# Transposing the queries by the DMA crossbar instead of TensorE, with tokens reordered and each head's means in its own 32 columns

## The chip, the cores and the metric

The kernel runs on one core of one Trainium2 chip. The metric is the device time of one execution, in microseconds (us). Before the change it is 233.38 us (median of 2 runs, 232.68 to 234.07). A ratio of two kernels is the mean time of one kernel's fast runs over that of the other's fast runs of the same rounds, so it is not quite the ratio of the medians quoted. A run counts as slow when it is over 1.5% above the fastest run of the same kernel.

The engines are called PE (TensorE, matmul), PEld (its weight loads), DVE (VectorE), ACT (ScalarE), POOL (GpSimd) and SP (SyncE; here it only issues DMA transfers).

## The reference, cut to what matters

```python
# q, k, v: (8 batches, 8 heads, 576 tokens, 64); phi: (8, 8, 576, 32)
a   = softmax of phi over the tokens            # 32 memories per head
k_m = einsum('bhsm,bhsd->bhmd', a, k)           # means of k
v_m = einsum('bhsm,bhsd->bhmd', a, v)           # means of v
x   = softmax(scale * q @ k_m^T) @ v_m          # attention over 32 memories
# heads side by side: x is (8, 576, 512); x_prev is x moved on by one token
xk  = mu_k * x + (1 - mu_k) * x_prev
xr  = mu_r * x + (1 - mu_r) * x_prev
out = sigmoid(xr @ w_r) * (relu(xk @ w_k)**2 @ w_v)    # 512 -> 1024 -> 512
```

Two things matter. The scores need q with the 64 features on the partitions, while the load brings it with tokens on the partitions, so q has to be transposed. And x_prev needs the previous token, so the order in which tokens lie in the columns decides which pieces are subtracted.

## The kernel before

Order is fixed by hand. The channel mix works through 9 chunks of 512 tokens, each of 16 groups of matmuls (8 groups of keys, called pk in the program; 4 of gates, pr; 4 of values, pv). The steps of the attention of later batches are placed between them: `("exp", -15)` puts the exponential of phi 15 groups before the chunk in which the batch is reckoned to begin. In the steady state one batch's steps lie beside one chunk. In the profiles, em is the exponential of phi, kvps the means of k and v, zps the sums that normalise, qtps the transposed queries in PSUM and qT their copy in SBUF, scps the scores, nops the values before the cast to x.

```python
STEADY = [("q2", -15), ("q0+pv", -15), ("q3+pk", -15), ("q1", -15), ("exp", -15), ("kv+pv", -14), ("z+pv",
          -14), ("nk", -13), ("nv", -13), ("load", -11), ("tk", -11), ("s3", -9), ("s1+pk", -9),
          # ... scores, denominators, values, differences, mixing
FIRST = { 0: [...], 1: [...], 2: [...], 3: [...] }    # places for the first four batches; cut

def exp_phi():                                  # "exp", on ACT; em is what the means wait for
    nc.scalar.activation(em[:, 0:NB].rearrange("p j h m -> p h j m"), L["phm"], AF.Exp)
    nc.scalar.activation(em[:NT, NB], L["pht"], AF.Exp)

# "kv": means of k and v, 20 matmuls, two heads (64 columns of PE) at a time
for j in range(NJ):
    for c in range(2):
        for jj in range(2):
            pr = 2 * c + jj
            nc.tensor.matmul(kvps[jj * 64:(jj + 1) * 64, c], lhsT=heads(j, pr * 64, 64),
                             rhs=kv5[:, parts, 2 * pr:2 * pr + 2, j, :], ...)

def tr_q(pr):                                   # "q0" to "q3": queries transposed on PE, 40 matmuls a batch
    def go():
        ps = ps_tile([128, NJ * 128], BF16, "qtps")
        for j in range(NJ):
            for i in range(2):
                nc.tensor.matmul(ps[i * D:(i + 1) * D, j * 128:(j + 1) * 128],
                                 lhsT=q5[:, 2 * pr + i, j, :], rhs=identity, is_transpose=True, ...)
        nc.vector.tensor_copy(st["qT"][:, pr, :], ps[:, 0:S])
    return go

def values(c, hf):                              # "x0" to "x3": nops on PE, then the cast to x on ACT
    ...
            nc.scalar.copy(st["x"][:, 2 * c + jj, sl], pss[jj])

def store(o, t, cols):                          # output stores; SP issues them, in program order
    eng = nc.sync
    ...
    eng.dma_start(out=dst, in_=o[p:p + n, cols])
```

All loads after the first phi (phi, k, q, v of each batch, and the weights) go through one queue that POOL issues; batch b + 2 is loaded while batch b is worked on. POOL issues each load when the buffer that it overwrites has come free.

The softmax here doesn't subtract the row's maximum and nothing guards it: scores larger than these inputs give would overflow.

## Time and profile before

| | before |
|---|---|
| median us (2 runs) | 233.38 |
| span of the profiled run, us | 231.6 |
| PE / ACT / DVE busy, share of the span | 94% / 70% / 62% |
| first key matmul (pk) | 23.3 us |
| length of a chunk, first key to first key, chunks 0 to 8 (the last ends the kernel) | 32.6, 26.5, 22.5, 22.7, 22.8, 22.7, 18.6, 17.3 and the rest |

The page of the kernel before shows, in 40 equal slices of the span, busy tenths of PE and the mean of the 16 DMA engines; then the queue of SP's transfers (packets, MB, share of the 16 engines' span); then two groups of instructions (partitions by columns, elements, type, count, then busy us, mean ns, idle us before them and what ended most of it).

```profile
PE   7688999789999999999999999999999999999990
DMA  6999999999999999992899300420023043023033
q1 hardware_dynamic: 7008, 9.77, 14.5%
L292 PE MATMUL qtps<-identity,q 128*64 128x128 bf16 x320 | 13.4, 233 | 1.5 <-DMA q<-in_q_dram 1.4
L238 PE MATMUL kvps<-kv,em 128*64 128x256 bf16 (+1 forms) x200 | 10.8, 254 | 1.6 <-DMA kv<-in_k_dram 1.6
```

The reader should see that PE hardly rests, that the DMA engines are full for the first half (20 slices of 5.8 us) and then mostly free, and that the two groups which the change removes or halves cost PE 13.4 and 10.8 us.

### The profile page before, as it was taken

Reading aid. Unit: us, or ns where it says so; the run is one execution under the profiler, and the core shown is the slowest. Engines: PE = TensorE matmul, PEld = TensorE weight load, DVE = VectorE, ACT = ScalarE, POOL = GpSimd, SP = SyncE. Lnnn points to the kernel's source line nnn. Section 1 sums busy time; section 2 is a strip of 40 time slices with the busy share of each in tenths; the row PEclk is TensorE's granted clock in tenths of the full one; section 3 lists DMA queues with packets and bytes.
Section 4 is the critical chain, followed back from the end, with each engine's and each line's share of the span. In section 5 each row is a group of like instructions: output and inputs, shape, how many; then the busy total and the mean of one; then the engine's idle time right before and its main releaser. Section 6 shows DMA issues by size and latency. Waiting matters only on the chain.

```text
span 231.6 us, 4343 instructions
## 1 busy us (share of the span) xinstructions
PE 217.9 (94%) x1649; PEld 108.4 (47%) x1649; DVE 142.6 (62%) x353; ACT 161.2 (70%) x305; POOL 54.1 (23%) x74
## 2 busy tenths in 40 slices
PE   7688999789999999999999999999999999999990
PEld 3344444355435455445444774464444444444450
DVE  3436744396467896588638966896687767425222
ACT  3116688852986894998599859976988865765860
POOL 8573451553455508101900000000000000000000
PEclk9958999999999999999999999999999999999998
DMA  6999999999999999992899300420023043023033
GB/s 134 190 197 213 224 200 224 196 237 245 213 226 193 255 207 261 189 220 96 159 178 165 91 3 0 93 91 0 3 92 91 1 93 91 0 92 91 3 91 91
DMA packets 49365, 31.49 MB, mean 136 GB/s; under 512 B 14920, under 2 KB 43856, under 8 KB 49344
## 3 DMA queue, kind: packets, MB, share of 16 engines
q0 software_dynamic: 41520, 20.91, 64.9%
q1 hardware_dynamic: 7008, 9.77, 14.5%
q10 hardware_dynamic: 816, 0.52, 0.9%
q8 instruction: 13, 0.21, 0.4%
q14 instruction: 8, 0.07, 0.1%
HBM read 38.54 MB, written 9.44 MB: 207 GB/s over the span
## 4 chain that ended last, share of the span: by engine, by line
PE 78%; DMA 10%; ACT 5%; DVE 3%; issue 1%; POOL 1%; DVEq 0%; POOLq 0%
PE pk L480 25%; PE pv L513 24%; PE pr L494 13%; DMA q<-in_q_dram 10%; PE qtps L292 4%; PE kvps L238 3%; PE nops L346 2%; PE scps L306 2%; PE zps L319 1%; ACT sg L501 1%; ACT sg L502 1%; DVE atn L333 1%; ACT sg L499 1%; PE zps L248 1%; ACT e L309 1%
## 5 line engine op out<-in xcount | busy, mean ns | idle before, releaser
L480 PE MATMUL pk<-xkT,wk 128*128 128x512 bf16 (+1 forms) x320 | 67.2, 358 | 0.2 <-ACT xrT L409 0.2
L513 PE MATMUL pv<-wv,sq 128*128 128x512 bf16 (+1 forms) x296 | 66.2, 373 | 0.0
L484 ACT ACTIVATE rl<-pk 128x512 bf16<-128x512 f32 x72 | 42.8, 598 | 29.6 <-PE pk L480 29.6
L485 DVE TENSOR_TENSOR sq<-rl 128x512 bf16<-128x512 bf16 x72 | 29.8, 424 | 28.0 <-ACT rl L484 27.6
L515 DVE TENSOR_TENSOR o<-sg,pv 128x512 f32<-128x512 f32 (+1 forms) x37 | 23.9, 672 | 32.5 <-ACT sg L502 25.2
L513 PEld LDWEIGHTS <-sq 128*128 128x128 bf16 x296 | 28.6, 98 | 32.3 <-issue 0.7
L480 PEld LDWEIGHTS <-wk 128*128 128x128 bf16 x320 | 29.9, 98 | 28.1 <-issue 0.8
L494 PE MATMUL pr<-wr,xrT 128*128 128x512 bf16 x144 | 35.5, 380 | 0.0
L499 ACT ACTIVATE sg<-pr 128x512 f32<-128x512 f32 x36 | 22.0, 614 | 8.9 <-PE pr L494 8.9
L494 PEld LDWEIGHTS <-xrT 128*128 128x128 bf16 x144 | 12.8, 98 | 15.1 <-issue 2.3
L501 ACT ACTIVATE sg<-sg 128x1024 f32<-128x1024 f32 x18 | 19.0, 1057 | 0.6
L502 ACT ACTIVATE sg<-sg 128x1024 f32<-128x1024 f32 x18 | 19.0, 1057 | 0.6
L309 ACT ACTIVATE e<-scps 128x288 bf16<-128x288 f32 x32 | 11.6, 445 | 9.8 <-PE scps L306 9.7
L296 DVE COPY qT<-qtps 128x576 bf16<-128x576 bf16 x32 | 13.1, 452 | 6.8 <-PE qtps L292 6.6
L350 ACT CAST x<-nops 128x288 bf16<-128x288 f32 x48 | 16.8, 423 | 0.0
L371 DVE TENSOR_SCALAR mu_d<-diff,mu 128x576 bf16<-128x576 bf16 x48 | 15.5, 364 | 0.0
L292 PE MATMUL qtps<-identity,q 128*64 128x128 bf16 x320 | 13.4, 233 | 1.5 <-DMA q<-in_q_dram 1.4
L321 ACT ACTIVATE lz<-zps 128x288 f32<-128x288 f32 x32 | 11.4, 410 | 3.2 <-PE zps L319 3.2
L292 PEld LDWEIGHTS <-q 128*64 128x64 bf16 x320 | 10.6, 116 | 5.8 <-DMA q<-in_q_dram 2.6
L333 DVE TENSOR_TENSOR atn<-e,lz 128x576 bf16<-128x576 bf16 x16 | 12.0, 752 | 2.0 <-ACT lz L326 1.8
L107 POOL DMA_DIRECT2D phm<-in_phi_dram x7 | 6.3, 896 | 27.4 <-ACT em L222 24.4
L238 PE MATMUL kvps<-kv,em 128*64 128x256 bf16 (+1 forms) x200 | 10.8, 254 | 1.6 <-DMA kv<-in_k_dram 1.6
(67 smaller groups left out, 211.8 us busy)
## 6 DMA issues: line engine op xcount, KB each, us to landing
out_dram<-o SPq DMA_DIRECT2D x37, 128.0 KB, 2.4
kv<-in_k_dram POOLq DMA_DIRECT2D x8, 512.0 KB, 11.3
out_dram<-o SPq DMA_DIRECT2D x16, 256.0 KB, 2.7
phm<-in_phi_dram POOLq DMA_DIRECT2D x7, 512.0 KB, 11.9
q<-in_q_dram POOLq DMA_DIRECT2D x7, 512.0 KB, 12.2
kv<-in_v_dram POOLq DMA_DIRECT2D x7, 512.0 KB, 12.5
wk<-in_moe_w_k_dram POOLq DMA_DIRECT2D x2, 512.0 KB, 10.0
wv<-in_moe_w_v_dram POOLq DMA_DIRECT2D x1, 1024.0 KB, 15.6
```

Of the source, the lines that this page charges most:

```text
L238: nc.tensor.matmul(kvps[jj * 64:(jj + 1) * 64, c], lhsT=heads(j, pr * 64, 64), rhs=kv5[:, parts, 2 * pr:2 * pr + 2, j, :], start=j == 0 an ...
L292: nc.tensor.matmul(ps[i * D:(i + 1) * D, j * 128:(j + 1) * 128], lhsT=q5[:, 2 * pr + i, j, :], rhs=identity, is_transpose=True, start=True ...
L350: nc.scalar.copy(st["x"][:, 2 * c + jj, sl], pss[jj])
L480: nc.tensor.matmul(pk[:, lo:hi], lhsT=wk_sb[:, di, fi * 128:(fi + 1) * 128], rhs=xk_T[:, di, c0:c0 + hi - lo], start=(di == 0), stop=(di = ...
L484: nc.scalar.activation(rl, pk, AF.Relu)
L485: nc.vector.tensor_mul(st["sq"][:, fi, :], rl, rl)
L494: nc.tensor.matmul(pr, lhsT=xr_T[:, di, c0:c0 + 128], rhs=wr_sb[:, di, :], start=(di == 0), stop=(di == ND - 1))
L499: nc.scalar.activation(sg[:, ts % 2], pr, AF.Exp, scale=-1.0)
L501: nc.scalar.activation(sg, sg, AF.Ln, bias=1.0)
L502: nc.scalar.activation(sg, sg, AF.Exp, scale=-1.0)
L513: nc.tensor.matmul(pv[:, cols], lhsT=st["sq"][:, fi, ts * 128:(ts + 1) * 128], rhs=wv_sb[:, fi, cols], start=(fi == 0), stop=(fi == NF - 1))
L515: nc.vector.tensor_mul(o[:, cols], st[ts // 2][:, ts % 2, cols], pv[:, cols])
```

## The change

It has three parts. The queries are transposed by a DMA transfer that SP issues (`qx`), SBUF to SBUF through the crossbar of the DMA hardware: one for 128 rows of four tokens each, one for the last 64 tokens, 16 rows. This frees PE of 40 matmuls and DVE of 4 copies a batch. A row of the transfer holds pairs of tokens, so the columns of a batch come out with even tokens first, then odd; blocks are now of 144 tokens, and differences, masks and stores follow this order. And the means use 32 columns of PE for a head, four heads at once, so that nothing is computed for the wrong head.

```diff
-STEADY = [("q2", -15), ("q0+pv", -15), ("q3+pk", -15), ("q1", -15), ("exp", -15), ("kv+pv", -14), ...
+STEADY = [("qx", -17), ("exp", -15), ("kv+pv", -14), ("z+pv", -14), ("nk", -13), ...
# FIRST likewise: qx at -57, 5, -4 and -12 for batches 0 to 3; cut
+def load_q(b):        # q's main part as before, its tail as 16 rows of four tokens; no halves for batch 0
-                for j in range(NJ):
-                    for c in range(2):
-                        for jj in range(2):
-                            pr = 2 * c + jj
-                            nc.tensor.matmul(kvps[jj * 64:(jj + 1) * 64, c], lhsT=heads(j, pr * 64, 64),
-                                             rhs=kv5[:, parts, 2 * pr:2 * pr + 2, j, :],
+                for j in range(NJ):
+                    for h in range(H):
+                        c, g = divmod(h, 4)
+                        nc.tensor.matmul(kvps[g * M:(g + 1) * M, c], lhsT=em[:, j, h, :],
+                                         rhs=kv5[:, parts, h, j, :],
-        def tr_q(pr):     # 10 transposes on PE and a copy on DVE, four times; cut
+        def tr_q():
+            st["qT"] = work.tile([128, H, 2, S // NB], BF16, name="qT", tag="qT")
+            qT = st["qT"].rearrange("p h j t -> p (h j) t")
+            nc.sync.dma_start_transpose(out=qT[:, :, 0:128], in_=qs[b % 2].rearrange("p h j d -> p (h j d)"))
+            nc.sync.dma_start_transpose(out=qT[:, :, 128:], in_=qts[b % 2].rearrange("p h j d -> p (h j d)"))
# scores: 4 matmuls of 32 columns in place of 2 of 64; normalising, differences, mixing and
# stores in the new order of tokens; cut
```

## The prediction

> **What bounds the kernel now.** The page has PE busy 94% of the span, ACT 70%, DVE 62%, but such shares average over stages, so I read busy time by stretch first. Columns: stretch, length, then busy us (instructions) of PE, PE weight loads, DVE, ACT, POOL; granted clock, DMA, GB/s.
>
> ```profile
> 23.30:45.00 21.70, 20.43 (x184) 9.94 (x184) 10.36 (x29) 16.88 (x33) 8.87 (x12) 1.00 1.44 211
> 45.00:64.00 19.00, 16.91 (x200) 9.29 (x194) 13.47 (x37) 10.91 (x27) 8.46 (x11) 1.00 1.44 229
> 64.00:88.00 24.00, 23.44 (x223) 12.03 (x224) 18.90 (x44) 19.77 (x41) 10.73 (x14) 1.00 1.48 219
> 110.00:132.00 22.00, 22.00 (x176) 11.52 (x170) 15.17 (x37) 17.65 (x36) 5.51 (x8) 1.00 0.97 156
> 132.00:155.00 23.00, 23.00 (x198) 13.23 (x198) 16.77 (x41) 18.64 (x37) 0.00 (x0) 1.00 0.17 47
> ```
>
> The reader is to see two regimes. From about 72 us PE never rests, so PE time removed there is worth its length unless another engine takes over. Before 64 us PE rests 2.1 us in a 19 us stretch while DMA is full: loads share the pace. The chain of waits says the same:
>
> ```profile
> 2.93 9.07 DMA q<-in_q_dram
> 50.55 12.94 DMA q<-in_q_dram
> 129.43 0.23 PE nops L346 x2
> 129.66 1.24 PE qtps L292 x40
> 130.90 0.98 PE pk L480 x8
> 131.88 0.23 PE nops L346 x2
> 132.11 1.21 PE kvps L238 x20
> 133.32 0.34 PE zps L248 x10
> ```
>
> Start, length, what. Queries are awaited twice (batch 0 and batch 3); later it is PE alone, and of a batch's period (129.66 less 106.94 is 22.7 us) the transposes take 1.24 us and the means of k and v 1.21 us. Then I looked at what ACT does while PE transposes, because the means need its exponential em:
>
> ```profile
> 129.96 0.70 ACT L350 CAST x<-nops 128x288 bf16<-128x288 f32 x2
> 130.53 1.08 ACT L221 ACTIVATE em<-phm 128x1024 bf16<-128x1024 f32 x1
> 131.49 0.41 ACT L222 ACTIVATE em<-pht 64x256 bf16<-64x256 f32 x1
> ```
>
> The main em ends at 131.6 and its means start at 132.1: only 0.45 us apart. At batch 4 it is 0.2 us, at batches 5 and 7 about 0.4. The transposes hide em.
>
> **What the Trainium skill says.** (1) TensorEngine Tiling (Array Packing), section Tiling Modes: column tiles of one array work in parallel, and a change of tiling mode drains it. The trace agrees: two matmuls on different 64-column halves start 2 to 3 ns apart, pairs of 128 columns follow every 56 ns, pairs of 256 every 109 ns, and a block in another mode costs about 0.1 us more (20 x 56 ns is 1.12, the block takes 1.24). (2) VectorE: DVE Perf Modes, section The three transpose paths: a 128x128 bf16 transpose is 390 ns on TensorE and 1309 ns by the DMA crossbar. For PE the measured figure here is far less in a stream: 40 halves in 1.24 us. (3) DMA: Bandwidth & Descriptors, section Latency and other measured facts: a transpose by DMA with a non-contiguous middle dimension ran at 261 GB/s. No run here shows it yet. (4) The same page, section Queues, rings and completion order: each DMA engine takes turns between queues packet by packet. So the new transfers slow the load stream they sit beside.
>
> **The change part by part.**
> *PE transposes.* 40 matmuls and weight loads per batch go: 1.24 us of PE at batches 4 to 7, 13.4 us busy in all. 4 DVE copies of 452 ns per batch go as well, 13.1 us busy in all; DVE is not the bound, so alone they are worth nothing late.
> *Means.* 20 matmuls of 64 by 256 columns become 40 of 32 by 128. Ten pairs of 109 ns become ten quads. If four column quarters run together as two halves do, a quad costs 56 ns: 10 x 56 + 0.12 = 0.68 us in place of 1.21, gain 0.53. Scores: 2 pairs of 288 columns become 2 quads of 288 (122 ns each before), no change. Differences: pieces of 1536, 508, 256 and 4 elements (958 + 420 + 290 + 169 = 1837 ns) become 1152, 576, 572 and 4; by the line through the first two (about 154 ns + 0.52 ns an element) 757 + 456 + 453 + 169 = 1835 ns, no change.
> *Sum on PE in the steady state:* 1.24 + 0.53 = 1.77 us a batch. But PE then reaches the means at about 127.69 + 3.16 us (keys 0 and 1 1.73, nops 0.23, key 2 0.97, nops 0.23), and em ends 3.96 after that start, since ACT cannot begin it before the casts of the first nops, which do not move. So PE waits 0.86 us, and the means end at 4.02 + 0.68 = 4.70 in place of 5.59: **0.9 us gained a batch, not 1.77**. Batch 4, where em is later (its end is 86.46, the means began 86.64), gains 0.12 + 0.53 = 0.65. Four batches: 3 x 0.9 + 0.65 = **3.4 us**.
> *Start.* Half of q(0) landed at 12.04, and scores began at 14.77, the second set at 18.2 because PE was transposing. Now the whole q(0) must land (about 13.5, between the landings of the old halves, 12.04 and 13.78) and then 576 KB must pass the crossbar. At 261 GB/s this is 2.3 us, doubled by turns with the load stream, plus some 2 us of completion as the 2.4 us of an output store shows: estimate 5.5 us, so qT at about 19. All four scores then come at once; after them ACT has 4 exp of 0.36, 4 logs of 0.35 and 2 of 0.68 us, 4.2 us in a row, then DVE 0.75 and the mixing. First key at about 25.7 against 23.25: **2.5 us lost**, if PE is not slowed further by its idle clock (0.71 granted in this stretch already). This is absorbed: 50 us into the kernel PE has saved batch 1's transposes (1.4), its means (0.7) and batch 2's first transposes (1.3), so it stands about 0.9 us ahead and then waits for v(2).
> *Loads.* The trace's landings show a stream without gaps from 1 to 104 us: v(2) at 54.2, v(3) at 67.2, a batch some 11 to 13 us. Each transpose delays it by T. From 2.3 us at the quoted rate, of which part overlaps, I estimate T = 1.7 to 2.6. The loads gain 0.3 us a batch from q's tail in 512 B instead of 128 B pieces, and lose a wait of about 0.7 us for PE before q(2). So v(2) lands 2T - 1.5, about 2 to 3.7 us, later. From v(2) to the means of batch 3 (54.2 to 70.6) PE loses 2.2 us of transposes, waits for q(3) and means, and v(3) must land, so about 1.9 us is won back there, and 0.5 in the means themselves: net between -0.5 and +1.3 us at 72 us.
> *Stores.* 144-token blocks give 69 output stores from the SP queue in place of 55, and 16 transposes stand among them. An output buffer has three copies, and a transpose is issued before the last value group of a chunk; a hold of a few us reaches nobody.
> *Sum:* -3.4 late, and +0.4 (-0.5 to +1.3) early: 233.4 - 3.0 = 230.4.
>
> **Rivals.**
> 1. *Everything on PE counts.* 7 batches x 1.77 = 12.4 us, less 2.5 for the start: 223.5. For it: PE 22.00 of 22.00. Against it: em, 0.45 us behind, and DMA full until 104 us.
> 2. *The crossbar is slow.* If 1309 ns per 128x128 block holds one after another, 16 blocks and the tail are over 22 us a batch. From the issue to the scores lie about 12 us in the steady state (v3 to scps), so PE would wait some 10 us at each of four batches, and the start would lose 17: 265 or more. If it is half as slow, about 11 us, only the start and the loads lose: 237. For it: no measurement in this trace. Against it: the skill's second figure, and that 16 DMA engines can take a block each.
> 3. *The load stream becomes the bound until batch 3.* With T = 5, v(2) lands 8.5 us later, of which 2.4 are won back and 3.4 later: 236. For it: DMA 9 tenths in the first half. Against it: T of 5 would be twice my estimate.
> 4. *Quads don't run together* (four 32-column weight loads in a row): 40 x 28 ns + 0.12 is 1.24, nothing gained in the means. That costs 4 x 0.53: 232.5.
>
> **Range and chances.** The middle lies near 230.5. Rival 1 in part gives the low end, 225; rivals 2 (mild) and 3 the high end, 239. The limit for faster is 228.7: it needs both a quick crossbar and em not in the way, 0.27. Slower begins at 238: a slow crossbar, 0.2. Within: 0.53.
>
> **What would show it.** In the changed profile: no qtps; kvps x40 at about 0.68 us in the chain; PE idle before kvps released by em, about 0.8 us in each of batches 5 to 7 (if absent, the gain a batch is 1.77 and I am wrong on the main step); the time from SP's issue of a transpose to the first scps, about 5.5 us at the start; first pk near 25.7; v(2) landing at 56 to 58 with PE waiting there; a batch's period of 21.8 us late in the kernel. A period above 22.7 late, or scps released by the transpose there, makes the prediction wrong upward.

## The result, and the profile after

| | before | after |
|---|---|---|
| median us (2 runs each) | 233.38 (232.68 to 234.07) | 263.24 (261.52 to 264.96) |
| ratio of fast runs | | 1.128 (95%: 1.0932 to 1.1628) |
| span of the profiled run, us | 231.6 | 263.2 |
| first key | 23.3 | 39.8 |
| chunk lengths 0 to 7 | 32.6, 26.5, 22.5, 22.7, 22.8, 22.7, 18.6, 17.3 | 30.0, 28.0, 37.1, 26.1, 22.2, 22.1, 18.6, 17.3 |

The change made the kernel 13% slower. The chunk starts say where: 16.5 us are lost before the first key, 2.6 are won back in chunk 0, 1.5 lost in chunk 1, 14.6 lost in chunk 2 (beside batch 4's attention), 3.4 lost in chunk 3 (batch 5's), 0.6 won in each of chunks 4 and 5. The sum is 32.2, beside 31.6 us between the two spans.

The page after, the same rows as before with the granted clock of PE added; the group is that of the scores, which read the transposed queries:

```profile
PE   8600099967976898305998699899899999999992
PEclk9955579999999999955999899999999999999998
DMA  6999999999999999999929993502802302204122
q1 hardware_dynamic: 24352, 14.72, 27.6%
L309 PE MATMUL scps<-qT,kmT 64*32 64x288 bf16 x128 | 6.6, 328 | 39.5 <-DMA qT<-qt 37.1
```

PE has two holes now, in the third to fifth and the 17th to 19th slice (of 6.6 us each), and its granted clock is down to half in both; after the first it needs one more slice to come back. SP's queue went from 7,008 packets to 24,352: 17,000 more for only 5 MB more. Of the 58.3 us that PE is idle, 39.5 stand before the scores, and a transpose ended 37.1 of them. The waits of PE (what waited, for what, us in all, times, longest) give the same in one line and show the smaller waits:

```profile
PE scps L309 <- DMA qT<-qt: 37.1, 4, 20.4
PE kvps L247 <- ACT em L231: 4.7, 5, 1.3
PE zps L257 <- ACT x L353: 0.9, 3, 0.3
```

The four waits are 20.4 us at batch 0, 13.5 at batch 4, and 1.9 and 1.3 at batches 2 and 3; before batch 5's scores there are 2.2 us more, for which the view names no releaser; the tail of batch 5's transpose landed 0.1 us before they began (147.26 and 147.35). The chain of waits after (start, length, what) at batch 0 and at batch 4:

```profile
21.17 11.60 DMA qT<-qt
32.91 0.44 PE scps L309 x8
...
108.10 13.02 DMA qT<-qt
121.20 0.67 PE scps L309 x8
```

SP's own timeline after (start, length, what, count; the length of a store's group includes SP waiting for the output to be ready) shows when each transpose was issued:

```profile
13.41 7.66 SPq L297 DMA_TRANSPOSE qT<-q  x1
21.17 1.16 SPq L298 DMA_TRANSPOSE qT<-qt  x1
...
88.95 12.55 SPq L462 DMA_DIRECT2D out_dram<-o  x8
101.61 6.40 SPq L297 DMA_TRANSPOSE qT<-q  x1
...
163.24 2.64 SPq L297 DMA_TRANSPOSE qT<-q  x1
```

At batch 0 SP issues at once: q lands at 13.39 by the trace's landing events, and the issue starts at 13.41. Still the main part lands only at 32.38 and the tail at 32.77. At batch 4 there are two delays. q had landed by 93.3, but SP issues in order and stood behind 8 output stores until 101.6. Then the transpose takes as long as at batch 0: the tail lands at 121.11. The DMA view gives the median time from issue to landing of the main and the tail transposes:

```profile
qT<-q SPq DMA_TRANSPOSE x8, 13.8
qT<-qt SPq DMA_TRANSPOSE x8, 9.3
```

The median hides two cases. While loads run (batches 0 to 4) the main part takes 19.0, 16.1, 14.3, 13.3 and 19.3 us; when they have ended (batches 6 and 7) 4.8 and 6.5 us. Batch 5 lies between: its packets passed in a gap of the loads, but the loads that began again at once delayed its completion (7.3 us) and its tail. The records of single packets say why. A main transpose is 2,048 packets of 256 B; shared evenly that is 128 on each of 16 engines (the records do not name the engine). Beside loads, as many load packets pass as transpose packets: 2,073, 2,025, 2,112, 2,095 and 2,149 load packets between the first and the last of the 2,048, the 4-byte records of completions not counted. From first packet to last takes 14.4, 11.6, 9.6, 8.5 and 13.9 us, which divided by 128 is 113, 90, 75, 66 and 109 ns a turn; the mean load packet in those stretches lasts 101, 77, 63, 56 and 97 ns. On average a turn is one load packet and some 10 to 13 ns. In the same time the loads moved 1.7 to 4.1 times the bytes of the transpose, so the two did not share by bytes. Without loads 2,048 packets pass in 2.6 to 4.0 us over all runs (e4's pieces apart), 20 to 31 ns a turn. In front of this stands the issue: the first packet comes 3.9 to 4.4 us after it beside loads, 1.2 to 1.3 us in an unloaded stretch.

Busy time by stretch after (stretch, length, busy us and count of PE, PEld, DVE, ACT, POOL, granted clock, DMA, GB/s): the two holes, and a steady stretch late in the kernel. DMA is the summed time of the packets as a share of 16 engines; it passes 1 because packets overlap.

```profile
12.00:33.00 21.00, 0.54 (x10) 0.30 (x10) 0.48 (x2) 0.00 (x0) 8.00 (x11) 0.51 1.36 191
100.00:122.00 22.00, 7.47 (x87) 3.34 (x86) 5.10 (x16) 6.47 (x15) 3.77 (x5) 0.76 1.53 167
183.00:205.00 22.00, 20.89 (x161) 9.37 (x159) 15.01 (x37) 18.10 (x37) 0.00 (x0) 1.00 0.32 75
```

In the first two the DMA engines are as busy as in the full stretches before (1.36 and 1.53 beside 1.44), but the core computes little, or next to nothing. In the last PE rests 1.1 us of 22, where it had no rest before. PE's timeline there shows why (in brackets, idle time before it and what ended it):

```profile
187.21 0.74 PE L247 MATMUL kvps<-kv,em 128*32 128x128 bf16 x40 [0.81 <-ACT em L231]
188.25 0.39 PE L257 MATMUL zps<-ones,em 128*128 128x1 bf16 x10 [0.30 <-ACT x L353]
```

The means take 0.74 us for 40 matmuls (the prediction said 0.68), after a wait of 0.81 (predicted 0.86), and a second wait of 0.30 follows, for ACT's casts of the values, which free the PSUM buffer that the next sums are to use.

### The profile page after: what moved, and what is told of

Same layout as the page of the kernel before. It is cut to its first block, busy times and chain, and to the rows that moved or that the text cites.

```text
span 263.2 us, 4220 instructions
## 1 busy us (share of the span) xinstructions
PE 204.9 (78%) x1577; PEld 94.3 (36%) x1577; DVE 129.7 (49%) x319; ACT 160.9 (61%) x305; POOL 52.2 (20%) x73
## 3 DMA queue, kind: packets, MB, share of 16 engines
q1 hardware_dynamic: 24352, 14.72, 27.6%
## 4 chain that ended last, share of the span: by engine, by line
PE 48%; DMA 27%; ACT 11%; DVE 4%; issue 4%; SPq 3%; POOL 1%; DVEq 0%; POOLq 0%
PE pk L481 17%; PE pv L514 15%; DMA qT<-qt 13%; PE pr L495 10%; DMA qt<-in_q_dram 6%; DMA qT<-q 5%; DMA q<-in_q_dram 4%; SPq L297 3%; ACT sg L502 2%; ACT sg L503 2%; PE scps L309 2%; ACT sg L500 2%; ACT rl L485 1%; ACT x L353 1%; DVE o L516 1%
## 5 line engine op out<-in xcount | busy, mean ns | idle before, releaser
L514 PE MATMUL pv<-wv,sq 128*128 128x512 bf16 (+1 forms) x296 | 66.9, 376 | 0.0
L495 PE MATMUL pr<-wr,xrT 128*128 128x512 bf16 x144 | 37.4, 396 | 0.0
L309 PE MATMUL scps<-qT,kmT 64*32 64x288 bf16 x128 | 6.6, 328 | 39.5 <-DMA qT<-qt 37.1
L500 ACT ACTIVATE sg<-pr 128x512 f32<-128x512 f32 x36 | 21.8, 608 | 11.5 <-PE pr L495 11.5
L309 PEld LDWEIGHTS <-kmT 64*32 64x32 bf16 x128 | 1.9, 92 | 42.8 <-issue 37.8
L362 DVE TENSOR_TENSOR diff<-x 128x1152 bf16<-128x1152 bf16 x6 | 4.5, 758 | 23.3 <-ACT x L353 23.3
L126 POOL DMA_DIRECT2D q<-in_q_dram x8 | 7.1, 884 | 27.7 <-DMA qT<-qt 16.0
L205 PE MATMUL idle<-zeros 128*128 128x512 bf16 x32 | 11.0, 499 | 1.2 <-DVE zeros L144 1.2
```

Source lines behind the costliest of these rows:

```text
L309: nc.tensor.matmul(ps[m, :], lhsT=st["kmT"][r, c, m], rhs=st["qT"][r, 4 * c + g].rearrange("p j t -> p (j t)"), start=True, stop=True, ski ...
L495: nc.tensor.matmul(pr, lhsT=xr_T[:, di, c0:c0 + 128], rhs=wr_sb[:, di, :], start=(di == 0), stop=(di == ND - 1))
L500: nc.scalar.activation(sg[:, ts % 2], pr, AF.Exp, scale=-1.0)
L514: nc.tensor.matmul(pv[:, cols], lhsT=st["sq"][:, fi, ts * 128:(ts + 1) * 128], rhs=wv_sb[:, fi, cols], start=(fi == 0), stop=(fi == NF - 1))
```

## The experiments

**Theory.** A transpose of many small packets takes its turn behind the load stream packet for packet, so it lands 13 to 19 us after its issue as long as loads run, and 5 to 7 us after it otherwise; where it is issued late, SP's order adds to this. **Rivals.** The crossbar itself is slow (a fixed cost, loads or not); the loads are what is late, and the transpose only shows it; or the loss comes from the reordering or the narrow means.

### e1_means_alone: only the narrow means, in the kernel before

```diff
 # kernel before; kvps [128, 2, w, D], normalised with v or k broadcast over both halves and the mask
-                    for c in range(2):
-                        for jj in range(2):
-                            nc.tensor.matmul(kvps[jj * 64:(jj + 1) * 64, c], lhsT=heads(j, pr * 64, 64), ...
+                    for h in range(H):
+                        c, g = divmod(h, 4)
+                        nc.tensor.matmul(kvps[g * M:(g + 1) * M, c], lhsT=em[:, j, h, :], ...
```

> The kernel before with only the means changed to 40 matmuls of 32 columns each; queries still go through PE, columns keep the old order. Theory: a quad of 32-column tiles runs in the time of one (56 ns), so a batch's kvps block is 0.68 us in place of 1.21 us, and as nothing waits for em here (the transposes still hide it) 7 or 8 batches gain about 0.5 us: 229.5 us, range 228.5 to 231. Rival (weight loads of the quarters go one after another): block 1.2 us or more, 233 to 234 us.

Measured: 231.19 us (230.69 to 231.91, 4 runs), ratio 0.9891 (0.9848 to 0.9934), 0.2 us above the expected range. The result is correct. The block of means in PE's timeline:

```profile
108.98 0.74 PE L237 MATMUL kvps<-kv,em 128*32 128x128 bf16 x40
```

So this part is good: four heads side by side cost 0.74 us where two took 1.28 at the same place of the kernel before, a chunk is 0.4 us shorter, and the kernel gains 1.1%. It agrees with the Trainium skill, TensorEngine Tiling (Array Packing), section Tiling Modes, that tiles work independently, here for four column tiles. The loss does not come from here.

### e2_before_noload: the kernel before, without the loads after batch 1

```diff
-                load_batch(b + 2)
+                loads[b + 2] = loads[b]
```

The result is wrong: later batches work on old data.

> The kernel before, with no loads after batch 1 (batches 2 to 7 reuse the data of 0 and 1, so the result is wrong on purpose). It is the base for the next run. PE waited about 2 us for loads of batches 2 and 3, so about 230 to 232 us.

Measured: 233.37 us (1 run). Expected was a small gain, and there is none in the total, so this is a miss. The trace shows why one run can't settle it: the first key came 1.4 us later here (24.6 for 23.3), at a place where the loads are the same, and from there on the kernel took 207.0 us in place of 208.4. So the later loads cost the kernel before at most some 1.4 us, less than the start differs from run to run. The rival "the loads are what is late" would need more than that.

### e3_after_noload: the changed kernel, without those loads

The edit is the same, and the result is again wrong.

> The kernel after, with the same loads left out (wrong on purpose). Theory C (the crossbar's packets take turns with the load stream on the 16 DMA engines): from batch 2 on a transpose of 128 rows lands within 5 to 7 us of its issue as the two late ones of the kernel after did (4.8 and 6.5 us), no wait of scores for qT is left after batch 1, the start is as slow as in the kernel after (first key at about 39 us, 16 us late), and from then on it gains about 1 us a batch on the run beside it: about 239 to 243 us, 8 to 12 us over it. Theory Q (the transposes are issued too late in the order of SP's queue, behind stores) or theory X (the crossbar is slow by itself): waits of 5 to 20 us before scores remain at batches 2 to 4, 255 us or more.

Measured: 242.06 us (1 run), a hit. PE's waits for a transpose, and the median landing of the eight main ones:

```profile
PE scps L309 <- DMA qT<-qt: 19.8, 1, 19.8
qT<-q SPq DMA_TRANSPOSE x8, 6.1
```

Only batch 0's long wait is left, where the first loads still run. From batch 2 on the main transposes land in 4.8 to 6.9 us and the scores wait at most 0.2 us; chunks late in the kernel take 22.1 us. The same transposes with loads beside them cost 21 us more (263.2 to 242.1), so the crossbar by itself is not slow.

### e4_split32: the main transpose in four pieces

```diff
-            nc.sync.dma_start_transpose(out=qT[:, :, 0:128], in_=qs[b % 2].rearrange("p h j d -> p (h j d)"))
+            for r in range(0, 128, 32):
+                nc.sync.dma_start_transpose(out=qT[:, :, r:r + 32],
+                                            in_=qs[b % 2][r:r + 32].rearrange("p h j d -> p (h j d)"))
```

This asked whether another cut of the transfer changes its packets. Pieces of 16 rows were meant first, but such a kernel does not build: the build accepts an operand of the transpose only at partition 0, 32, 64 or 96.

> The kernel after, with the transpose of 128 rows cut into four of 32 rows. In the trace of after the 128-row one moves in 2048 packets of 256 B a batch, the 16-row tail in 16 of 4096 B. Theory C says that turns are taken packet by packet, so time under load goes with the number of packets: if 32 rows go in larger packets than 256 B, landing under load falls from 13 to 19 us to half or less and the kernel to 240 to 250 us; if the packets stay at 256 B, landing stays at 13 to 19 us and the time within 258 to 268 us. Theory X: the same landing either way.

Measured: 273.12 us (1 run), above the 258 to 268 expected for packets that stay as they are.

```profile
PE scps L311 <- DMA qT<-qt: 41.2, 3, 20.6
```

The packets stay 2,048 of 256 B, so nothing is gained, and SP has four issues in place of one. Fewer and larger packets could not be had in this way; whether another layout would give them stays open. So no run changed the size of the packets: that their number decides is read from the records, not shown by an edit.

### e5_noload_hold: e3, and the loads after batch 0's queries held until its transpose has landed

```diff
 # transposes of batch 0 issued right after load_q(0), then on POOL, before the load of v(0):
+    held = const.tile([128, 2], BF16, name="held")
+    nc.gpsimd.tensor_copy(held[:, 0:1], qT0[:, 0, 0, 0:1])
+    nc.gpsimd.tensor_copy(held[:, 1:2], qT0[:, 0, 0, 143:144])
```

The two copies of one column make POOL, which issues the loads, wait for the transposes. The result is wrong, as in e3.

> The kernel after without loads after batch 1 (wrong on purpose, as in the run it is compared with, 242.06 us), and with all loads behind q(0) (v, weights, batch 1) held back on POOL until batch 0's qT has landed. Theory C: the first transpose then has the DMA engines to itself: it lands 5 to 7 us after its issue at about 12.5 to 13.5 us, and its tail by 20 us in place of 32 us; the weights come later (both halves of wk by about 27 us), first key at about 27 to 30 us in place of 39 us, and the time 231 to 236 us. Theory X (the crossbar or SP's issue is slow at the start for another reason): qT still lands near 30 us and the time gets worse, over 250 us.

Measured: 243.53 us (1 run). The time is a miss, the mechanism a hit.

```profile
PE psmu L217 <- DMA mu<-in_moe_mu_r_dram: 11.4, 1, 11.4
PE scps L318 <- DMA qT<-qt: 10.2, 1, 10.2
```

The first transpose is issued at 13.45 and lands at 18.13, 4.7 us later, and the tail at 18.53 in place of 32.1 in e3. The first key comes at 30.3 in place of 39.1. It could hardly come earlier: the first half of its weights, held back too, landed only at 29.6, and a side effect of the edit put the loads of mu behind the transposes on SP (first line). And the held loads come later, so batch 1's transpose is the one that is awaited now (second line), landing at 54.04. Taking the loads out of the transpose's way at the start is possible but paid nothing here, since the same bytes are needed soon after.

### e6_after_early: the changed kernel with the transpose issued five positions earlier

```diff
-STEADY = [("qx", -17), ("exp", -15), ...
+STEADY = [("qx", -22), ("exp", -15), ...
```

> The kernel after with one number changed: in batches 4 to 7 the transposes are issued five positions earlier in the order (before two of a chunk's four output stores in place of after them all). Theory Q (order of SP's queue): batch 4's q had landed 8 us before its transpose was issued, so the wait for it falls by up to 8 us: about 255 us. The waits at batches 0 and 2 (issue within 0.1 us of the landing of q) cannot change. If contention alone decides, the transpose is only slowed as much earlier: 260 us or more.

Measured: 245.54 us (1 run), more gained than expected (255).

```profile
PE scps L309 <- DMA qT<-qt: 21.6, 2, 20.5
92.18 6.04 SPq L297 DMA_TRANSPOSE qT<-q  x1
```

Batch 4's transpose is issued at 92.18 (second line, from SP's timeline), once q has landed, and its tail lands at 106.00; its wait is gone. From batch 5's means to batch 6's it now takes 22.2 us in place of 26.1, so what batch 5 lost is gone as well. Some 18 of the 30 us were therefore the place of the issue in SP's order at batch 4, with what followed from it: a transpose of 14 us can be hidden if it starts 14 us ahead. At the start there is nothing to hide it behind.

### e7_hybrid4: batches 0 to 3 transposed on PE, 4 to 7 by the crossbar

The layout and the means are those of the changed kernel; batch 0's q is loaded in two halves again. Where loads run from the start, PE transposes, in blocks of 128x128 (two tokens of one head together); the crossbar is used from batch 4 on.

```diff
-STEADY = [("qx", -17), ...                    # changed kernel
+STEADY = [("qx", -21), ...
 # FIRST: q0 to q3 at the places of the kernel before, and "qt" for the 16-row tails
+                for i in range(2):
+                    for jp in range(2):
+                        nc.tensor.matmul(
+                            ps[:, i, jp, :],
+                            lhsT=qs[b % 2][:, 2 * pr + i, 2 * jp:2 * jp + 2, :].rearrange("p j d -> p (j d)"),
+                            rhs=identity, is_transpose=True, start=True, stop=True, skip_group_check=True)
+                nc.vector.tensor_copy(qT[:, 2 * pr:2 * pr + 2, :, 0:128], ps)
```

> The kernel after, but queries of batches 0 to 3 are transposed on PE (positions of the kernel before) and those of batches 4 to 7 by the crossbar, issued 10 positions before their scores. Column order and means as in after. Theory C: loads of batches 0 to 3 are undisturbed and the start is as in the kernel before (first key near 23 us); from batch 4 on no scores wait for qT, the means wait about 0.9 us for em in each of batches 4 to 7. Against the run with the means alone (231.2) it gains 1.24 - 0.86 = about 0.4 us a batch for four batches, and loses up to 1 us for the separate tail transposes: 229.5 us, range 228 to 232.

Measured: 229.24 us (228.32 to 230.48, 4 runs), ratio 0.9839 (0.9801 to 0.9876), a hit. The kernel is 34 us faster than the changed one with the same order of tokens, stores and means, so the loss is not theirs; what differs is who transposes in the first four batches, and when SP issues for the others. What PE waits for most is now what the prediction named:

```profile
PE kvps L254 <- ACT em L238: 3.4, 4, 1.0
```

### e8_hybrid4_exp: e7 with the exponential of phi two positions earlier

```diff
-STEADY = [("qx", -21), ("exp", -15), ...
+STEADY = [("qx", -21), ("exp", -17), ...
```

> As e7_hybrid4, with the exponential em of batches 4 to 7 two positions earlier in ACT's order (before the relu of the chunk's first two keys). Theory E (em takes the place of the transposes as the wait before the means): the wait of 0.9 us falls to 0.3 or less and 4 x 0.6 us are gained on e7: 227 us, range 226 to 229. Rival: ACT only passes the delay on to the relus and so to the next keys: no gain, within 0.5 us of e7.

Measured: median 234.39 us (230.17 to 235.73, 20 runs, of which only 5 count as fast, since one run at 230.17 sets the limit); ratio of the fast runs 0.9978 (0.9942 to 1.0014). This is a miss. The profiled run was a slow one, so the lengths that follow, and the granted clock of 0.78 from 104 to 127 us, only say what happened in it. The wait for em is gone and late chunks take 21.1 and 21.0 us, as hoped, but chunk 3 takes 30.0:

```profile
PE scps L344 <- DMA qT<-qt: 6.2, 2, 5.9
```

Batch 5's transpose runs from 98.72 to 115.5, beside the loads of batch 7. My reading is that the earlier exponential frees the buffer of phi earlier, so POOL starts the next batch's loads earlier, and these now meet the transpose. e11 and e12 test it.

### e9_hybrid4_exp16: e7 with the exponential one position earlier

```diff
-STEADY = [("qx", -21), ("exp", -15), ...
+STEADY = [("qx", -21), ("exp", -16), ...
```

> As e7_hybrid4 with em one position earlier (between the first two keys of a chunk) in place of two. Theory E: e8 lost its gain not on ACT but because an earlier em frees phi's buffer earlier, so the load stream of batch 7 starts earlier and runs beside the crossbar's transpose of batch 5 (16.8 us in e8, 12.7 us in e7), and scores of batch 5 waited 5.9 us. At one position earlier the waits of means for em go (3.4 us in e7, to under 1), and a wait of scores for qT of batch 5 of 0 to 6 us may remain: 226.5 to 231 us. Rival (ACT passes the delay on to relus and keys): keys wait for relu 0.8 us or more a batch, and no wait of scores for qT: 229 us or more.

Measured: 228.79 us (228.04 to 229.84, 4 runs), ratio 0.9816 (0.9768 to 0.9865). The wait for em is gone here too, but most of it comes back in two other places:

```profile
PE scps L344 <- DMA qT<-qt: 2.6, 2, 1.4
PE zps L264 <- ACT x L388: 2.4, 3, 0.8
```

The exponential now runs before the casts that free the PSUM buffer of zps, so that wait grows from 0.3 to 0.8 us a batch. A late chunk takes 21.8 us.

### e10_hybrid4_best: e9, and batches 5 to 7 transposed six positions earlier

```diff
+for _b in (5, 6, 7):
+    FIRST[_b] = [("qx", -27)] + STEADY[1:]
```

> As e9_hybrid4_exp16, and the transposes of batches 5 to 7 are issued six positions earlier (about 8 us). Theory C with E: no scores wait for qT any more, no means for em, so the whole 1.24 us of the transposes is gained in four batches: 229.2 less 3.4, 226 us, range 225 to 227.5, about 3% under the kernel before. If ACT is in the way (rival), 228.5 us or more.

Measured: 230.38 us (229.33 to 232.94, 4 runs, one slow), ratio 0.9864 (0.9821 to 0.9907). This is a miss; it is no better than e9.

```profile
PE kvps L256 <- DVE o L554: 1.7, 1, 1.7
```

SP waits at the early transposes for q to land (5.3 us the longer time), the output stores behind it wait too, and PE comes to wait for DVE's product that fills an output buffer. Issuing a transpose earlier than its data is there stops the stores.

### e11_exp17_early: e8 with the early transposes of e10

```diff
 # STEADY with ("exp", -17), and
+for _b in (5, 6, 7):
+    FIRST[_b] = [("qx", -27)] + STEADY[1:]
```

> e8_hybrid4_exp (234.4 us; its late periods are 21.1 us, but the one of batch 5 is 30.0 us) with the transposes of batches 5 to 7 issued six positions earlier. Theory: the 8.8 us lost in e8 are the wait for batch 5's qT, whose transpose ran beside the loads of batch 7. Issued about 8 us earlier it lands in time whatever runs beside it: period 21.1 to 22.5 us, time 225 to 228 us. Rival: the earlier transposes hold SP's queue and the output buffers (1.7 us of wait in e10): 229 us or more.

Measured: 229.40 us (228.16 to 231.85, 4 runs), ratio 0.9816 (0.9773 to 0.9858); the expected gain over e9 is not there. In its profile (a slow run) chunk 3 takes 26.5 us in place of e8's 30.0, and the wait for output buffers is 2.9 us. Both theories are right in part: the collision can be avoided by an earlier issue, and the earlier issue holds the stores.

### e12_pe5: e8 with batch 5 back on PE

```diff
 # STEADY with ("exp", -17) and ("qx", -21); batch 5 alone has PE transposes and its old place of exp
+FIRST[5] = [("q2", -15), ("q0+pv", -15), ("q3+pk", -15), ("q1", -15), ("qt", -15), ("exp", -15)] + STEADY[2:]
```

Only batches 4, 6 and 7 use the crossbar: batch 4's transpose is issued early enough to be hidden, and 6 and 7 come after the loads.

> e8_hybrid4_exp with batch 5 transposed on PE, the crossbar only for batches 4, 6 and 7, and em of batch 5 back in its place. Theory (collision of batch 5's transpose with batch 7's loads): no wait of scores for qT is left, batch 5's period is 22.3 us as in the run with the means alone, the others 21.1 to 22: 227 us, range 226 to 228.5. Rival (e8 was slow because em delays relus and keys, and the period of 30 us has another cause): over 230 us.

Measured: **226.94 us** (226.13 to 228.29, 4 runs), ratio 0.9733 (0.9688 to 0.9779), correct. It is a hit, the fastest kernel, and 2.7% under the kernel before; it alone has an interval that lies wholly beyond 2%. No score waits for a transpose by the crossbar. PE's timeline shows the means of batch 6 without a wait in front, and the scores too:

```profile
130.05 0.74 PE L255 MATMUL kvps<-kv,em 128*32 128x128 bf16 x40
135.95 0.43 PE L345 MATMUL scps<-qT,kmT 64*32 64x288 bf16 x8
```

The late chunks take 21.1 and 21.0 us, against 22.7 before: 1.6 or 1.7 us a chunk, close to the whole 1.77 that the prediction's first rival gave for PE time removed. Batch 4's transpose still takes 14.4 us, those of batches 6 and 7 some 5 us.

## Why the prediction was wrong

It said 230.5 us, with 225 to 239 as its range, and 263 came out. Step by step:

- **Start (2.5 us lost): this step failed.** It took the crossbar's time as 2.3 us by bytes, "doubled by turns with the load stream", plus 2 us of completion, and wrote 5.5 for it (by its own terms the sum is 6.6). The runs show 19 us. The failure is in pricing by bytes and then sharing in halves. The transfer is 2,048 packets of 256 B, and beside each passes, on average, one load packet, which is larger and slower; 128 turns of 113 ns are 14.4 us where the doubling gave 4.6, after 4.0 us until the first packet. e5, with no loads beside it, took 4.7 us, near 2.3 and 2; so the estimate was right for a transfer alone and wrong for one beside loads. What followed was as predicted: from qT to the first key 6.7 us were reckoned (19 to 25.7), and 7.0 measured (32.8 to 39.8). Nor was the loss "absorbed": only 2.6 of 16.5 us came back in chunk 0.
- **Stores ("a hold of a few us reaches nobody"): this failed too.** It looked at what a transpose does to the stores, not at what stores do to a transpose. At batch 4 it was issued 8 us after its data had landed, and with 14 us or more beside loads it could not be there for the scores: 14.6 us. e6 shows it, since five positions earlier took the wait away and 18 us off the kernel. (It counted 69 output stores; the trace has 64 from SP.)
- **Loads (net -0.5 to +1.3 us at 72 us):** PE waited 3.2 us at batches 2 and 3, and chunk 1 was 1.5 us longer. The place was right and the waiter was the scores, not the means. v(2) landed at 63.6, 9.4 us later than before and not 2 to 3.7, but the late start is in that too, and PE did not wait for it. Batch 5 lost another 3.4 us; POOL's issue of q waited once, 16.0 us, for batch 4's transpose, which had yet to read the old copy, and this delays later loads. I have not separated this loss from the late arrival at batch 4.
- **PE transposes and means, 0.9 us gained a batch:** the terms held, and the sum was too large. The wait for em was predicted as 0.86 and measured as 0.81, the means as 0.68 and 0.74. The gain of a late chunk was 0.6 (22.7 to 22.1). The term left out is the 0.30 us wait of zps for ACT's casts. With the 0.06 us by which the means took longer it is 0.36 of the expected 0.9. The reasoning that the transposes had hidden em is confirmed by e12: with em earlier a late chunk is 21.0 us.
- **Scores, differences, DVE copies:** no effect was predicted, and none is seen; the four differences take 758, 451, 452 and 168 ns, 1,829 in all beside 1,835 predicted.
- **Rivals.** The second, "the crossbar is slow", gave the right size of loss at the start (17 us) in its strong form, but for a reason that is false: alone a transpose passes in about 3 us. That its total (265 or more) lies near the measured one is luck: its own terms, 17 us and 10 at each of four batches, come to some 290, and one batch alone waited so long. What it held against itself, that the engines share the work, fits the records (2,048 packets of 23 ns passed in 2.8 us, so some 17 were under way at once) and did not help, because the loads were to pass on the same engines. Rival 3's delay of v(2) (8.5 us) is near the 9.4 measured, but the loss did not come by that way. Rival 4 fell (0.74 us for 40). Rival 1's gain per batch was reached only in e12, once em was moved.

Open: why e8's time scatters so, and how much of batch 5's loss has which cause. That the earlier exponential brings the loads forward was read from one trace and fits e11 and e12, but was not tested alone. In e8's profile the granted clock was 0.78 around the hole, against 1.00 in e7's; whether that makes the scatter is not shown.

## What to carry to other kernels

Price a DMA of many small packets, when another queue is loaded, by packets times the other queue's packet time, not by bytes (here 128 turns of 66 to 113 ns, 8.5 to 14.4 us), and add what it takes to start; and look at what stands ahead of it on the engine that issues it. A slow but hidden transfer costs nothing if it is issued early enough, and issued too early it holds whatever stands behind it, so use such a transfer for the stages in which the load stream has ended and keep the compute engine's own path for the others. After removing work from the bound engine, check what the removed work was hiding, and move that as well: here the removal alone took a late chunk from 22.3 us (e1) to 22.2 (e7), and with em moved to 21.1 (e12), but the move also freed a buffer and so started loads that met the transpose.

## What the Trainium skill lacked or had wrong

- DMA: Bandwidth & Descriptors, section Queues, rings and completion order: it says that engines switch queues at packets and that a packet holds some 9 to 17 descriptors. In the trace's records as many load packets as 256 B transpose packets pass (2,073 to 2,048), and no page prices what follows: 13 to 19 us beside loads for what takes 5 to 7 without.
- The same page, section Latency and other measured facts: 261 GB/s for a transpose with a non-contiguous middle dimension. Here 512 KB took 2.6 to 4.0 us from first to last packet without loads, 132 to 202 GB/s, and 36 to 62 GB/s beside loads (8.5 to 14.4 us).
- Advanced Engine Details and Errata, section X-Bar Transpose (TRN2): transposes "are as fast as regular DMAs". Alone that nearly holds here: 512 KB landed 4.8 us after the issue, the load of phi that SP issued first, of the same size, after 4.4. Beside loads it does not: in the time of one transpose (0.52 MB) the loads moved 0.9 to 2.15 MB.
- VectorE: DVE Perf Modes, section The three transpose paths: 1309 ns for a 128x128 block by the crossbar. In a stream of 16 blocks it is 0.16 to 0.25 us a block without loads, and 0.5 to 0.9 beside them. For TensorE its 390 ns is far above what a stream shows: 16 such blocks took 1.20 us in e12, 75 ns a block.
- I found no page with a time on this chip for it: the issue of a main transpose occupies SP for 1.9 to 3.0 us without loads and 4.8 to 7.9 us beside them, in which no store is issued.
- Nor on this: the build accepts an operand of a DMA transpose only at partition 0, 32, 64 or 96; pieces of 16 rows at partition 16 did not build.
